# Attention and feed-forward on one core: leaner elementwise work in batches 0 and 1, one long second pass over the weights' last half, and fewer unread products

## The chip, the core and the metric

The kernel runs on 1 core of a Trainium2 chip. The time is device microseconds for one execution. The median of the three runs shown is 1007.32 us (1006.21 to 1008.86).

A core has five engines with a queue each: TensorE (PE in the profile; PEld is its weight load), VectorE (DVE), ScalarE (ACT), GpSimd (POOL) and SyncE (SP, which here issues most DMA transfers). Each queue is worked in the order in which the program was written. TensorE writes to PSUM, eight banks of 512 float32 columns; GpSimd does not touch PSUM in this kernel.

## What is computed

```python
# attention, for 8 batches x 8 heads, 576 tokens, 64 columns a head
q_d, k_d, v_d = (mean of q, k, v over each 4 rows)          # 144 rows
out_d = softmax(q_d @ k_d.T / 8) @ v_d                      # down-sampled part, repeated 4 times
scores = where(|i - j| < 4, q @ k.T / 8, -1e9)
out = repeat(out_d, 4) + softmax(scores) @ v                # local part in a band of 7
# feed-forward, on x = out as 4608 tokens x 512
h = x @ w_in                                                # 512 -> 2048
y = (h * cos(h)) @ w_out                                    # 2048 -> 512
```

Products of the feed-forward part are done in three passes with operands that are split into a high and a low half (names ending in `h` and `l`).

## The kernel before

**Feed-forward.** The 4608 tokens are 12 tiles of 384 (`t`), the 2048 hidden columns 16 chunks of 128 (`c`). A step (t, c) is `gemm1` (L727: 12 matmuls at L739 into one of two banks, then the activation on ScalarE and VectorE, L748 to L757, and the low half of its result at L399) and, two steps later, `gemm2` (L763: nine matmuls at L775 into three banks that collect over chunks). Tile 0 is made of batch 0's tokens alone; tile 1 holds the last 192 tokens of batch 0 and the first 192 of batch 1; tile 2 the rest of batch 1. `PASSES` (L36) sets the order of the steps: tiles 0 to 2 go through chunks 0 to 3, then 4 to 7, 8 to 11 and 12 to 15, since the weights are still arriving; from tile 3 on, each tile goes through all 16. At the end of each pass of a tile its three banks are evacuated (L791); the first pass stores its result, the later ones add to it with an accumulating DMA from GpSimd's queue (L800).

**Weights.** `w_load` (L402) brings 64-bit words, 512 KB for a chunk of one matrix; `w_split` (L412) makes the two float32 halves: one step on ScalarE (L420), four on VectorE (L421, L423, L425, L427), the high half (L431 or L432) and the low half (L399). 32 such splits are made. The buffers of the last chunks first hold data of the attention of batches 0 and 1.

**Attention** works on pairs of heads, four in a batch, in five functions. `u_qk` (L469) loads q and k and sums groups of four rows (L490 on VectorE, or L483 and L485 on GpSimd). `u_v` (L494) loads v in two layouts and sums its groups of four rows (L504, L505, on GpSimd or VectorE). `u_s` (L510) makes the scores and the softmax: local scores (L546) and down-sampled scores (L555) in two banks; VectorE adds the mask (L569), takes the maximum (L574) and subtracts it (L399); the down-sampled maximum is L582; ScalarE does the exponentials (L593 to L597); sums and reciprocals follow (L609 to L613), and the scaling by them at L615, on GpSimd or VectorE, or at L621 on ScalarE in four steps. `u_t` (L626) transposes: local on VectorE (L632), down-sampled on TensorE (L648) with evacuations at L465 or L466. `u_pv` (L654) multiplies by v: down-sampled at L665, local at L677 (L684 from batch 2 on); L696 adds the two, and L711 and L399 write the high and low half of x. The functions have another branch for batches from 2 on (`b >= NEARLY`).

**What sets the order.** No queue's order is written by hand. `Plan` collects all operations with an engine (or several), an assumed length and their dependencies, and a list scheduler (L165 to L279) sets them in an order and picks the engine. After that, where TensorE is assumed idle before an operation, the loop at L885 puts in products that nobody reads (L892, of 512 columns, bf16); in front of batch 0's operations at least `CFG["warm"]` of them. SyncE's loads for batches 0 and 1 and the weights are in a chain written by hand (L858), with three in flight at first.

## Time and profile before

| what | value |
|---|---|
| median of the runs shown | 1007.32 us |
| the profiled execution's own time | 1007.4 us |
| its span, first to last instruction | 1005.6 us |
| mean granted TensorE clock | 0.988 |
| PE, DVE, ACT, POOL busy | 981.2, 681.7, 610.2, 221.3 us |
| unread products (L892) | 125, 38.7 us busy |
| accumulating stores on GpSimd's queue (L800) | 27 of 256 KB |

The profile is one execution, recorded by instruction. Busy time of TensorE includes pipelining and unread products, so that 98% does not say that all of it was needed. "Idle before" with a name behind it is the time for which an engine stood, and the instruction that let it go on. "issue" is a wait for nothing that the profile shows. A matmul on float32 data leaves two records. In the chain of waits, an instruction is counted from where its predecessor in the chain ended, so its piece may be shorter than its duration in the timeline.

### The profile page before, as it was taken

To read this page: it belongs to the slowest core of one execution; us is meant where nothing else is said; L and a number is where in the kernel's file an instruction comes from. 1 tells how busy PE (TensorE), PEld (TensorE's weight loads), DVE (VectorE), ACT (ScalarE), POOL (GpSimd) and SP (SyncE) were. 2 spreads that over 40 slices of the span, in tenths; PEclk is the share of its full clock that TensorE was granted. 3 is DMA by queue.
4 is the path that set the end of the run, shared out by engine and by line. 5 is a ranking of instruction groups with operands and counts; after the bars stand their busy time and mean duration, and the time that the engine had idled before them with its cause. 6 is when DMAs were issued, how large, how long until landed. Compare 5 with 4: busy or idle time off the path is not lost.

```text
span 1005.6 us, 23855 instructions
## 1 busy us (share of the span) xinstructions
PE 981.2 (98%) x9917; PEld 847.3 (84%) x9917; DVE 681.7 (68%) x1362; ACT 610.2 (61%) x1174; POOL 221.3 (22%) x280
## 2 busy tenths in 40 slices
PE   8878999999999999999999999999999999999998
PEld 4546899899887888889888888888888888899997
DVE  7799899986587578464758957655657865433433
ACT  3457588876576656555547746654646665655554
POOL 6775325631153202000002211200001300000000
PEclk9979799999999999999999999999999999999999
DMA  7784643424355322210212312201112320100000
GB/s 224 234 270 149 215 159 64 80 36 68 67 116 132 78 65 70 68 33 28 81 49 71 129 49 58 83 26 36 62 54 73 112 65 4 37 1 1 32 1 32
DMA packets 41051, 80.70 MB, mean 80 GB/s; under 512 B 4976, under 2 KB 16240, under 8 KB 40944
## 3 DMA queue, kind: packets, MB, share of 16 engines
q1 hardware_dynamic: 37056, 72.11, 23.2%
q0 software_dynamic: 3888, 7.08, 5.0%
q8 instruction: 78, 1.28, 0.5%
q14 instruction: 29, 0.24, 0.1%
HBM read 57.93 MB, written 16.52 MB: 74 GB/s over the span
## 4 chain that ended last, share of the span: by engine, by line
PE 87%; DVE 6%; DMA 4%; issue 1%; ACT 1%; SPq 0%; ACTq 0%; DVEq 0%
PE bank L775 38%; PE bank L739 38%; PE bank L539 2%; PE bank L684 2%; PE bank L555 2%; PE bank L665 2%; PE bank L648 1%; DMA q<-qT 1%; DMA wdi<-w_in 1%; PE bank L892 1%; PE bank L677 1%; DMA vl<-vl 1%; DVE su L609 1%; DMA wxi<-qT 0%; DVE wxo L615 0%
## 5 line engine op out<-in xcount | busy, mean ns | idle before, releaser
L775 PE MATMUL bank<-wo,gh 128*128 128x512 f32 x1152 | 363.5, 396 | 0.0
L775 PEld LDWEIGHTS bank<-wo,gh 128*128 128x128 f32 x1152 | 210.0, 188 | 38.0 <-issue 3.1
L775 PE MATMUL bank<-wo,gl 128*128 128x512 f32 x576 | 227.6, 396 | 0.0
L750 ACT ACTIVATE tr<-bank,bmagic 128x384 f32<-128x384 f32 x192 | 110.9, 577 | 113.5 <-PE bank L739 109.7
L754 DVE SCALAR_TENSOR_TENSOR tr<-tr,bank 128x384 f32<-128x384 f32 x192 | 105.0, 547 | 108.0 <-ACT tr L749 107.1
L751 DVE SCALAR_TENSOR_TENSOR tr<-tr,bank 128x384 f32<-128x384 f32 x192 | 105.6, 550 | 84.2 <-ACT tr L750 83.2
L748 ACT ACTIVATE tr<-tr 128x384 f32<-128x384 f32 x192 | 100.7, 524 | 77.0 <-DVE tr L751 76.4
L756 ACT ACTIVATE gh<-tr 128x384 fp32r<-128x384 f32 x163 | 85.3, 523 | 88.3 <-DVE tr L754 86.8
L399 DVE TENSOR_TENSOR gl<-tr,gh 128x384 fp32r<-128x384 f32 x154 | 92.4, 600 | 63.5 <-ACT gh L756 60.5
L775 PEld LDWEIGHTS bank<-wo,gl 128*128 128x128 f32 x576 | 108.0, 187 | 23.5
L739 PE MATMUL bank<-x0h,wi 128*128 128x384 f32 x384 | 107.5, 340 | 0.0
L739 PE MATMUL bank<-x1h,wi 128*128 128x384 f32 x384 | 107.1, 339 | 0.0
L739 PE MATMUL bank<-x2h,wi 128*128 128x384 f32 x384 | 106.8, 338 | 0.0
L739 PE MATMUL bank<-x3h,wi 128*128 128x384 f32 x384 | 106.5, 338 | 0.0
L749 ACT ACTIVATE tr<-tr 128x384 f32<-128x384 f32 x192 | 100.8, 525 | 6.1
L399 POOL TENSOR_TENSOR gl<-tr,gh 128x384 fp32r<-128x384 f32 x38 | 43.0, 1132 | 269.6 <-DVE gh L757 175.8
L739 PEld LDWEIGHTS bank<-x0h,wi 128*128 128x128 f32 x384 | 70.5, 189 | 2.6 <-issue 0.5
L739 PEld LDWEIGHTS bank<-x1h,wi 128*128 128x128 f32 x384 | 70.3, 188 | 2.6 <-issue 0.6
L739 PEld LDWEIGHTS bank<-x2h,wi 128*128 128x128 f32 x384 | 70.2, 188 | 2.3 <-issue 0.4
L739 PEld LDWEIGHTS bank<-x3h,wi 128*128 128x128 f32 x384 | 70.2, 188 | 2.0
L739 PE MATMUL bank<-x0l,wi 128*128 128x384 f32 x192 | 64.6, 337 | 0.0
L739 PE MATMUL bank<-x3l,wi 128*128 128x384 f32 x192 | 64.6, 336 | 0.0
(199 smaller groups left out, 1452.6 us busy)
## 6 DMA issues: line engine op xcount, KB each, us to landing
vl<-vl SPq DMA_DIRECT2D x26, 384.0 KB
out<-ob SPq DMA_DIRECT2D x36, 256.0 KB
wdi<-w_in SPq DMA_DIRECT2D x16, 512.0 KB
wdo<-w_out SPq DMA_DIRECT2D x16, 512.0 KB
q<-qT SPq DMA_DIRECT2D x26, 292.0 KB
k<-kT SPq DMA_DIRECT2D x26, 292.0 KB
vd<-vdn SPq DMA_DIRECT2D x26, 288.0 KB
out<-ob POOLq DMA_DIRECT2D x27, 256.0 KB, 5.2
```

Of the source, the lines that this page charges most:

```text
L399: f = lambda e: lambda: e.tensor_tensor(out=out(), in0=in0(), in1=in1(), op=ALU.subtract)
L539: pe.matmul(banks[h].get()[BS * g:BS * (g + 1), c:c + BS], q.get()[hs, o:o + BS], k.get()[hs, o:o + BS], start=True, stop=True)
L555: pe.matmul(banks[h].get()[:HD, i * SD:(i + 1) * SD], qkd.get()[hs, 0, i * HD:(i + 1) * HD], qkd.get()[hs, 1, :], start=True, stop=True)
L665: pe.matmul(banks[0].get()[64 * h:64 * h + 64, 2 * SD:3 * SD], vd.get()[:, kh, 64 * h:64 * h + 64], ptd.get()[:, h, kh, :], start=(kh == 0 ...
L739: pe.matmul(ph.get()[:, :m], w[:, i, kc, :], x[:, kc, :], start=(n == 0), stop=(n == 3 * KC - 1))
L748: act.activation(tr.get(), tr.get(), AF.Sin, scale=PI)
L749: act.activation(tr.get(), tr.get(), AF.Square)
L750: pl.op("ACT", _act(m, True, 1), lambda: act.activation(tr.get(), h(), AF.Identity, bias=bmagic), r=[ph], w=[tr])
L751: pl.op("DVE", _dve(m), lambda: dve.scalar_tensor_tensor(out=tr.get(), in0=tr.get(), scalar=MAGIC, in1=h(), op0=ALU.subtract, op1=ALU.subt ...
L754: pl.op("DVE", _dve(m), lambda: dve.scalar_tensor_tensor(out=tr.get(), in0=tr.get(), scalar=0.5, in1=h(), op0=ALU.subtract, op1=ALU.mult), ...
L756: pl.op("ACT", _act(m, False), lambda: act.activation(gh.get(), tr.get(), AF.Copy), r=[tr], w=[gh], alts=[("DVE", _dve(m / 2), lambda: dve ...
L775: pe.matmul(o, (gh, gh, gl)[k].get()[:, sl], wo.get()[:, (0, 1, 0)[k]], start=(c == c0 and k == 0), stop=(c == c1 - 1 and k == 2))
```

## The change

All of it concerns batches 0 and 1, except `PASSES`.

- `PASSES`: tiles 0 to 2 now go through chunks 0 to 3, 4 to 7 and then 8 to 15 in one stretch.
- `warm` is 1 instead of 2: in front of batch 0's attention operations on TensorE stands at least one unread product.
- The mask is bf16, and TensorE puts it into the bank as a product with the identity ahead of the local scores, which are added to it. VectorE's mask addition goes; the maximum and the subtraction read PSUM, in halves of 192 columns, both on VectorE.
- The sum of v's groups of four rows goes; instead the down-sampled product takes all four rows of a group, in 16 matmuls where there were 4.
- The scaling of the down-sampled softmax is always on ScalarE.
- Three assumed lengths of the scheduler follow this (0.95 to 1.3, 0.64 to 2.1, and the scaling's).

```diff
-PASSES = [(t, c, c + NF) for c in range(0, NC, NF) for t in range(3)] + [(t, 0, NC) for t in range(3, NT)]
+PASSES = [(t, c, e) for c, e in ((0, NF), (NF, 2 * NF), (2 * NF, NC)) for t in range(3)] + [(t, 0, NC) for t in range(3, NT)]
...
-           fgap=0.4, f0=0.8, fend=300.0, warm=2)
+           fgap=0.4, f0=0.8, fend=300.0, warm=1)
...
-    mask = const.tile([P, NSEG + 1, BS], F32, name="mask")
+    mask = const.tile([P, NSEG + 1, BS], BF16, name="mask")
...
+        if b < NEARLY:
+            st[(b, pr)].update(vd=vd4, vl=vt)
+            return
         vd = ub(b, pr, "vd")
...
+            if b < NEARLY:
+                for h in range(2):
+                    pe.matmul(banks[h].get()[:, LQ:LQ + NSEG * BS], ident_b, mask[:, h:h + NSEG].rearrange("p s n -> p (s n)"),
+                              start=True, stop=False)
...
-                                  q.get()[hs, o:o + BS], k.get()[hs, o:o + BS], start=True, stop=True)
+                                  q.get()[hs, o:o + BS], k.get()[hs, o:o + BS], start=False, stop=(n % NSEG == NSEG - 1))
         if b < NEARLY:
-            pl.op("PE", 0.95, l_mm, r=[q, k], pw=banks, w=loc)
+            pl.op("PE", 1.3, l_mm, r=[q, k], pw=banks, w=loc)
...
+        if b < NEARLY:
+            for h in range(2):
+                mx = pl.buf(None)
+                using(banks[h], pl.op("DVE", _dve(NSEG * BS), lambda h=h: dve.tensor_reduce(
+                    out=segs(mxl, h), in_=lq(h), axis=AX.X, op=ALU.max), r=[loc[h]], pw=[mxl], w=[mx]))
+                using(banks[h], pl.op("DVE", _dve(NSEG * BS), lambda h=h: dve.tensor_tensor(
+                    out=segs(sml, h), in0=lq(h), in1=segs(mxl, h).unsqueeze(2).broadcast_to([P, NSEG, BS]), op=ALU.subtract),
+                    r=[loc[h], mx], pw=[sml]))
...
-                alts.append(("ACT", 4 * _act(SD, False, 1), scaled))
-            pl.op("POOL", _pool(size), f(pool), r=[su], w=[sm], alts=alts, shares=True)
+                pl.op("ACT", 4 * _act(SD, False, 2), scaled, r=[su], w=[sm])
+            else:
+                pl.op("POOL", _pool(size), f(pool), r=[su], w=[sm], alts=alts, shares=True)
...
+            if b < NEARLY:
+                for i in range(8):
+                    for h in range(2):
+                        pe.matmul(banks[0].get()[64 * h:64 * h + 64, 2 * SD:3 * SD], vd.get()[:, i, 64 * h:64 * h + 64],
+                                  ptd.get()[:, h, i // 4, :], start=(i == 0), stop=(i == 7))
+                return
...
-            pl.op("PE", 0.64, d_mm, r=[vd, ptd], pw=[banks[0]], w=[poo])
+            pl.op("PE", 2.1, d_mm, r=[vd, ptd], pw=[banks[0]], w=[poo])
```

In the changed program the lines have moved: the mask product is L538, the scores L553 and L562, the maximum and the subtraction L582 and L584, the down-sampled maximum L599, the scaling on ScalarE L638, the transposes L666, the down-sampled and the local product L684 and L701, the additions L720, `gemm1` and `gemm2` L763 and L799, the unread products L916.

More of the change, by code (lines that the diff above doesn't have):

```diff
@@ L567, in u_s @@
         pl.op("POOL", 0.15, lambda: pool.memset(su.get(), 1.0), w=[su])
-        for h in range(2):
-            using(banks[h], pl.op("DVE", _dve(NSEG * BS), lambda h=h: dve.tensor_tensor(
-                out=sml.get()[:, NSEG * h:NSEG * (h + 1)], in0=banks[h].get()[:, LQ:LQ + NSEG * BS].rearrange("p (s n) -> p s n", n=BS),
-                in1=mask[:, h:h + NSEG] if b < NEARLY else band, op=ALU.add), r=[loc[h]] + zeroed[:1], pw=[sml]))
         n = 2 * NSEG * BS
         bl = lambda t: t.unsqueeze(2).broadcast_to([P, 2 * NSEG, BS])
-        pl.op("DVE", _dve(n), lambda: dve.tensor_reduce(out=mxl.get(), in_=sml.get(), axis=AX.X, op=ALU.max), r=[sml], w=[mxl])
-        sub(n, sml.get, sml.get, lambda: bl(mxl.get()), r=[mxl], w=[sml])
+        segs = lambda t, h: t.get()[:, NSEG * h:NSEG * (h + 1)]
+        lq = lambda h: banks[h].get()[:, LQ:LQ + NSEG * BS].rearrange("p (s n) -> p s n", n=BS)
+        if b < NEARLY:
[8 more added lines that the diff above has]
+            for h in range(2):
+                using(banks[h], pl.op("DVE", _dve(NSEG * BS), lambda h=h: dve.tensor_tensor(
+                    out=segs(sml, h), in0=lq(h), in1=band, op=ALU.add), r=[loc[h]] + zeroed[:1], pw=[sml]))
+            pl.op("DVE", _dve(n), lambda: dve.tensor_reduce(out=mxl.get(), in_=sml.get(), axis=AX.X, op=ALU.max), r=[sml], w=[mxl])
+            sub(n, sml.get, sml.get, lambda: bl(mxl.get()), r=[mxl], w=[sml])
         mxd = sb("mxd", 2, [HD, 2, 2])
@@ L621, in scaled @@
                             act.activation(smd.get()[:, h, i], smd.get()[:, h, i], AF.Copy, scale=sud()[:, h, i:i + 1])
-                alts.append(("ACT", 4 * _act(SD, False, 1), scaled))
-            pl.op("POOL", _pool(size), f(pool), r=[su], w=[sm], alts=alts, shares=True)
+                pl.op("ACT", 4 * _act(SD, False, 2), scaled, r=[su], w=[sm])
+            else:
+                pl.op("POOL", _pool(size), f(pool), r=[su], w=[sm], alts=alts, shares=True)
         u["sml"], u["smd"] = sml, smd
@@ L662, in d_mm @@
         def d_mm():
+            if b < NEARLY:
+                for i in range(8):
+                    for h in range(2):
+                        pe.matmul(banks[0].get()[64 * h:64 * h + 64, 2 * SD:3 * SD], vd.get()[:, i, 64 * h:64 * h + 64],
+                                  ptd.get()[:, h, i // 4, :], start=(i == 0), stop=(i == 7))
+                return
             for kh in range(2):
```

## The prediction

> **What bounds the kernel now.** First the page: its busy table, and the chain that ended last.
>
> ```profile
> span 1005.6 us, 23855 instructions
> PE 981.2 (98%) x9917; PEld 847.3 (84%) x9917; DVE 681.7 (68%) x1362; ACT 610.2 (61%) x1174; POOL 221.3 (22%) x280
> PE 87%; DVE 6%; DMA 4%; issue 1%; ACT 1%; SPq 0%; ACTq 0%; DVEq 0%
> ```
>
> TensorE is on the chain for 87%, and the 6% of VectorE and 4% of DMA must lie where TensorE is not yet saturated. The chain of waits, asked for the first 115 us, shows where that ends.
>
> ```profile
> 32.56 0.25 PE bank L648 x4
> 34.05 0.54 PE bank L892 x2
> 34.59 1.52 PE bank L677 x96
> 106.19 1.82 PE bank L892 x4
> 108.00 1.37 PE bank L539 x91
> 109.38 1.17 PE bank L555 x8
> 110.54 2.46 PE bank L739 x12
> ```
>
> The first multiplication of token tile 1 starts at 110.54. It needs batch 1's attention, and four steps on tile 0 were already done by then. What TensorE still waits for after 115 us is, in the waits of PE:
>
> ```profile
> PE bank L684 <- DMA ptb<-sml: 1.5, 3, 0.9
> PE bank L648 <- DVE smd L615: 0.8, 1, 0.8
> PE bank L539 <- ACT ptd L465: 0.4, 1, 0.4
> ```
>
> That is 2.7 us in 890. So the time is 110.54 us of head, then fixed TensorE work; the change counts by what it does to 110.54, and by any new wait behind it. The busy time by stretch, cut where batch 0's last addition ends (46.84) and where batch 1's does (107.36); the columns are length, then busy us and instructions of PE, PEld, DVE, ACT and POOL, the granted clock, DMA share and GB/s:
>
> ```profile
> 0.00:46.84 46.84, 40.51 (x1033) 23.60 (x1035) 34.81 (x74) 18.68 (x65) 31.68 (x65) 0.96 0.76 232
> 46.84:107.36 60.52, 49.43 (x887) 34.70 (x888) 56.41 (x107) 37.94 (x97) 37.20 (x43) 0.86 0.66 212
> ```
>
> In the second stretch VectorE is busy for 56.4 of 60.5 us: it sets the pace. In the first it has 12 us free, and waits for TensorE at the end.
>
> **Batch 0.** The timeline shows TensorE from the first transposes, and VectorE's wait behind the last head pair.
>
> ```profile
> 18.34 0.42 PE L648 MATMUL bank<-ident,smd 72*72 72x72 f32 x4
> 36.83 0.56 PE L546 MATMUL bank<-k,q 64*32 64x32 f32 x40
> 37.68 0.68 PE L546 MATMUL bank<-k,q 64*32 64x32 f32 x56 [0.29 <-issue]
> 90.09 0.71 PE L665 MATMUL bank<-wxi 72*64 72x144 f32 x8
> 90.73 0.44 PE L739 MATMUL bank<-x0h,wi 128*128 128x384 f32 x1
> 43.95 0.29 ACT L465 ACTIVATE wxi<-bank 128x144 f32<-128x144 f32 x1 [3.94 <-PE bank L665]
> 44.27 0.46 DVE L696 TENSOR_TENSOR wxi<-bank,wxi 128x288 f32<-128x288 f32 x1 [4.24 <-ACT wxi L465]
> 46.39 0.45 DVE L696 TENSOR_TENSOR wxi<-bank,wxi 128x288 f32<-128x288 f32 x1
> ```
>
> The program order on TensorE near the end of batch 0, third head pair, before (L892 are the unread products, L665 the down-sampled product, L677 the local one, L546 batch 1's first scores):
>
> ```order
> L665 MATMUL bank<-wxi_200 64x144 x4
> L892 LDWEIGHTS ident_b
> L892 MATMUL bank<-ident_b 128x512
> ...
> L677 MATMUL bank<-wxo_390,wxi_502 64x24 x48
> ...
> L648 MATMUL bank<-ident,wxi_214 72x72 x4
> L546 MATMUL bank<-k,q 32x32 x48
> ```
>
> and now (L916, L684, L701 and L553 are the same four, L538 the new mask products):
>
> ```order
> L701 MATMUL bank<-wxo_395,wxi_554 64x24 x48
> L916 LDWEIGHTS ident_b
> L916 MATMUL bank<-ident_b 128x512
> L684 MATMUL bank<-wxi_202,wxo_487 64x144 x16
> ...
> L666 MATMUL bank<-ident,wxi_205 72x72 x4
> L538 LDWEIGHTS ident_b
> L538 MATMUL bank<-mask,ident_b 128x192
> ...
> L553 MATMUL bank<-k,q 32x32 x48
> ```
>
> The down-sampled product went from 4 matmuls to 16, behind the local one, with one unread product between steps instead of two. Four of these matmuls took 0.64 us (90.09 to 90.73), so 16 take at most 2.56; the lower bound is the transposes' rate, 4 records in 0.25, which makes 2.0 for 32 records. I take 2.3. A head pair then costs two transposes 0.50, four unread products at 0.27 (half of the 0.54 for two) 1.08, local 1.52, down-sampled 2.3: 5.4 us. Four pairs are 21.6; batch 1's first scores 1.2 (0.56 and 0.68), their mask products and one unread product 0.5 (no row has 192 columns; a 512-column one costs 0.27, so two masks lie between 0 and 0.54, and I take the proportion, 0.2): 23.3. Here nothing waits for the sum of the four value rows any more: it has gone from VectorE and GpSimd, where it stood in line ahead of the scalings that the transposes wait for. So I let TensorE run without a pause from 18.34, to 41.6. Then the evacuation of 0.3 and two additions of 0.9: batch 0 ends at 42.8, **4.0 us** before 46.84. At 2.0 per product it is 5.2, at 2.56 3.0, and with pauses like the 0.29 of `issue`, some of them in each pair, up to 2 less. The first mask products also wait until GpSimd has written the mask, which held nothing before; I cost that at 0, since 18.34 comes after the scores of all four pairs, and at about 1 if it doesn't hide.
>
> **Batch 1.** VectorE's order at the border before (L696 batch 0's last additions, L427/L399 weight splitting and low halves, L569 to L574 batch 1's first softmax):
>
> ```order
> L696 TENSOR_TENSOR wxi_568<-bank,wxi_560 128x3x96
> L427 SCALAR_TENSOR_TENSOR xxh<-wdi_385,xxh 128x512
> L427 SCALAR_TENSOR_TENSOR xxh<-wdo_449,xxh 128x512
> L696 TENSOR_TENSOR wxi_568<-bank,wxi_560 128x3x96
> L399 TENSOR_TENSOR wi_946<-xxh,wi_946 128x512
> L399 TENSOR_TENSOR wo_951<-xxh,wo_951 128x512
> L399 TENSOR_TENSOR x0l<-wxi_568,x0h 128x384
> L399 TENSOR_TENSOR x1l<-wxi_568,x1h 128x192
> L569 TENSOR_TENSOR sml<-bank,mask 128x192 x2
> ```
>
> and now (L720, L582, L584 and L599 are additions, maximum, subtraction and the down-sampled maximum):
>
> ```order
> L427 SCALAR_TENSOR_TENSOR xxh<-wdo_453,xxh 128x512
> L399 TENSOR_TENSOR x0l<-wxo_487,x0h 128x384
> L490 TENSOR_REDUCE qkd<-q 128x144
> L399 TENSOR_TENSOR wo_957<-xxh,wo_957 128x512
> L582 TENSOR_REDUCE mxl<-bank 128x6 x2
> L584 TENSOR_TENSOR sml<-bank,mxl 128x192 x2
> L490 TENSOR_REDUCE wxo_199<-wxo_820 128x144
> L720 TENSOR_TENSOR wxi_577<-bank,wxi_552 128x3x96 x2
> L599 TENSOR_REDUCE mxd<-bank 72x2
> ```
>
> Batch 1's first softmax has moved ahead of batch 0's last additions, into the 4.24 us in which VectorE stood. The costs in 46.84 to 107.36, by groups, and one single instruction of the timeline:
>
> ```profile
> L423 DVE TENSOR_SCALAR xxh<-xxh 128x512 int32<-128x512 int32 x8 | 5.7, 714 | 0.0
> L421 DVE TENSOR_SCALAR xxh<-xxh 128x512 f32<-128x512 f32 x8 | 4.0, 514 | 0.0
> L425 DVE SCALAR_TENSOR_TENSOR xxh<-wdo,xxh 128x512 int32<-128x512 int32 x4 | 3.3, 813 | 0.0
> L427 DVE SCALAR_TENSOR_TENSOR xxh<-wdo,xxh 128x512 int32<-128x512 int32 x3 | 2.0, 678 | 0.0
> L615 DVE TENSOR_TENSOR wxo<-wxo,su 72x576 f32<-72x576 f32 x1 | 2.8, 2806 | 0.0
> L615 DVE TENSOR_TENSOR wxi<-wxi,su 72x576 f32<-72x576 f32 (+1 forms) x3 | 2.6, 883 | 0.0
> L399 DVE TENSOR_TENSOR wxi<-wxi,mxl 128x384 f32<-128x384 f32 x2 | 2.4, 1189 | 0.0
> L569 DVE TENSOR_TENSOR wxi<-bank,mask 128x192 f32<-128x192 f32 x4 | 1.2, 348 | 1.4 <-PE bank L555 1.4
> L574 DVE TENSOR_REDUCE mxl<-wxi 128x12 f32<-128x384 f32 x2 | 1.1, 536 | 0.0
> L504 POOL TENSOR_TENSOR wxi<-wxi 72x512 f32<-72x512 f32 x2 | 3.2, 1600 | 4.3 <-DMA wxi<-vdn 4.3
> 80.20 0.41 DVE L423 TENSOR_SCALAR xxh<-xxh 128x512 int32<-128x512 int32 x1
> ```
>
> Gone from VectorE here: four scalings 5.4 (2.8 and 2.6, one of them a smaller one that moves to GpSimd), four subtractions 3.4 (2.4, and two at 0.5), eight mask additions 2.4 (twice the row), four maxima 2.1, low halves now done elsewhere about 1.4: 14.7. New: six maxima and six subtractions of 192 columns at the mask row's 0.35 (0.27 if a row's overlap with the next is taken off, 0.44 as the 288-column maximum), 4.2; and the order puts three more weight splits ahead of batch 1's end, 3 x (0.51 + 0.71 + 0.81 + 0.68) = 8.1; casts and one reduction 2.4: 14.7. So it is even: the time won is filled with splits that come due earlier.
>
> What remains is relief. One scaling cost 2.81 us beside GpSimd where three averaged 0.88. Five sums of value rows leave GpSimd, by the 1600 row and a second addition of some 0.8 at most 12 of its 37.2 us, a third. What staying rows lose to it (L423 at 0.71 where the single one took 0.41, 8 x 0.3, and by estimate as much again twice over in the other rows) is some 8 us; a third is **2.6 us**, bounds 0 and 5. [...]
>
> ScalarE gets three more scalings in four steps, beside 37.9 us busy of 60.5; the rows for it, and for TensorE at half clock:
>
> ```profile
> 57.09 1.33 ACT L621 ACTIVATE smd<-smd,su 72x144 f32<-72x144 f32 x4 [3.00 <-DVE su L613]
> 103.41 2.77 PE L677 MATMUL bank<-wxi,wxo 32*64 32x24 f32 x96
> 102.25 1.23 PE L665 MATMUL bank<-wxo 72*64 72x144 f32 x8
> 57.55 1.49 PE L648 MATMUL bank<-ident,smd 72*72 72x72 f32 x8 [4.02 <-ACT smd L621]
> 104.00:106.00 2.00, 2.00 (x84) 2.00 (x80) 1.02 (x3) 0.00 (x0) 0.00 (x0) 0.50 0.52 188
> ```
>
> The scalings are 3 x 1.33 = 4.0 us more on ScalarE, which is idle for 22; the transposes wait for each. Last, the tail from batch 1's last addition to 110.54 took 3.2 us, the three rows at 106.19 to 109.38, at a granted clock of 0.50 (last row). At full clock they would take half of the 4.4 us that they run for, which leaves 1.0 to 1.5 behind the last addition; I take half of that gain, **1.0 us**.
>
> **Sum.** 4.0 + 2.6 + 1.0 = 7.6. The profiled execution took 1007.4 (span 1005.6 and 1.8 around it; the median shown is 1007.32), so I predict **999.8**. Behind 110.54, nine accumulating stores and their nine evacuations go: they hang on no TensorE wait above, worth 0 (2.7 either way, the waits that are there).
>
> **Rivals.** (a) *VectorE stays as slow and ScalarE queues*: no relief, no tail gain, and each of batch 1's four scalings waits behind one split step of 0.67. Then 4.0 - 2.7 = 1.3: 1006.1. For it: VectorE at 93%. Against: GpSimd's third is certain. (b) *Half clock in batch 0*, the one that ends slower. With half the unread products TensorE may lose its clock. At half clock the local product takes 2.77 against 1.52, the down-sampled one 1.23 against 0.64, and 1.82 is four unread ones. A pair then costs 1.0 + 1.8 + 2.8 + 4.4 = 10.0 instead of 5.4, the whole chain 23.3 x 1.85, 19.8 more. If two thirds of it run so, 13.2 more less 7.6 is 5.6: 1013.0; it decides from 38% of the chain on. Against: the bigger product keeps TensorE busier. [...] (c) *Chunks 12 to 15 come too late*: tile 0 now wants chunk 12 at step 28, not 36. Eight splits at 2.7 us, were none done ahead, are 21.6 of waiting less 7.6: 1021.3; it decides where VectorE falls a whole lead behind. Against it: the order puts chunk 12's split behind 17 steps' activations, chunk 15's behind 26 of 31, and 110 to 222 us ran with VectorE at 103.3 of 112:
>
> ```profile
> 110.00:222.00 112.00, 112.00 (x717) 100.63 (x714) 103.30 (x190) 91.00 (x171) 47.73 (x46) 1.00 0.42 109
> ```
>
> There the order has 22 splits in 27 steps, (103.3 - 22 x 2.7) / 27 = 1.6 us a step for the rest; now it has 19 in 22 steps, 19 x 2.7 + 22 x 1.6 = 86.5 of 91.3, 95% against 92%: tight, with a lead of 5 to 11 steps.
>
> **Chances.** Forecast 0.65, from 993.5 (product at 2.0, relief 5, the whole tail 2, and some 1.7 of VectorE's 4.1 idle: 13.9) to 1004.3; rival (a) 0.18 and mixtures of it and (b) 0.02, within 0.3% (3.0 us, about what a measurement here can tell); (b) 0.11 and (c) 0.04 slower. Range 993.5 to 1007.5, which takes in (a) and leaves out (b) and (c).
>
> **What would show it.** Right: token tile 1's first product near 103; batch 0's last addition near 42.8; the 16-matmul product at 2.0 to 2.6; GpSimd at 25 of the stretch; the same 895 us behind. Wrong: granted clock under 0.9 before 42; L666 waiting for ScalarE's scaling; a wait of TensorE on a split between steps 24 and 33.

## The result, and the profile after

The changed program took 1015.26 us at the median of 20 executions (1003.05 to 1022.62), the program before 1005.09 us (20 executions, 1001.51 to 1012.01). The ratio is 1.005, 95% interval 1.0028 to 1.0072; executions over 1.5% above the fastest of the same program are left out of the ratios here and below (seven of these 20, the profiled one among them, and three of e10's six), and the other 13 have a median of 1011.2. So it is slower. The 20 times go with TensorE's mean granted clock: 1003.05 at 0.995, 1005.45 at 0.990, 1009.39 at 0.987, 1014.09 at 0.980, 1020 to 1022.6 at 0.972 to 0.975.

The page of the profiled execution (1022.5 us):

```profile
span 1020.7 us, 24129 instructions
PE 1000.7 (98%) x10085; PEld 868.7 (85%) x10085; DVE 673.4 (66%) x1363; ACT 610.5 (60%) x1187; POOL 186.7 (18%) x236
```

VectorE lost 8.3 us of work and GpSimd 34.6, as the change intends; TensorE is 19.5 us busier, with 29 fewer unread products before its first step on tile 0 (44 for 73). The stretches, cut as before at the last additions of batches 0 and 1 (columns as there: length, busy us of PE, PEld, DVE, ACT, POOL, clock, DMA share, GB/s):

```profile
0.00:66.70 66.70, 59.21 (x1117) 42.56 (x1118) 33.47 (x84) 22.71 (x77) 17.70 (x47) 0.68 0.65 194
66.70:121.60 54.90, 50.59 (x970) 37.95 (x968) 51.64 (x116) 39.73 (x106) 25.01 (x25) 0.94 0.66 219
```

Batch 0 ends at 66.70 instead of 46.84 (+19.9), batch 1's stretch takes 54.9 instead of 60.5 (-5.6). Tile 1's first product starts at 123.89; the tail before it is 2.3 instead of 3.1, and what follows is 896.8 for 895.1. The sum, +15.1, is the difference of the spans. Batch 0 loses more than the whole of it, at a granted clock of 0.68. TensorE there:

```profile
18.43 0.96 PE L553 MATMUL bank<-wxo,wxi 64*32 64x32 f32 x89 [1.48 <-issue]
20.51 0.41 PE L666 MATMUL bank<-ident,smd 72*72 72x72 f32 x4
24.83 2.34 PE L701 MATMUL bank<-sml,vl 32*64 32x24 f32 x78 [2.77 <-issue]
27.64 4.11 PE L684 MATMUL bank<-ptd,vd 72*64 72x144 f32 x32
34.80 2.77 PE L701 MATMUL bank<-wxi,wxo 32*64 32x24 f32 x96
63.64 1.24 PE L562 MATMUL bank<-qkd 64*72 64x144 f32 x8
64.81 2.74 PE L916 MATMUL bank<-ident_b 128*128 128x512 bf16 x6
```

The down-sampled product takes 4.11 us and the local one 2.77; rival (b) had them at 4.4 and 2.8. Behind the first transposes (20.51) a pause of 2.77 us for `issue` (which no instruction released) stands inside a local product. VectorE's softmax of batch 1, which the order had moved ahead, came no earlier:

```profile
64.95 0.36 DVE L584 TENSOR_TENSOR sml<-bank,mxl 128x192 f32<-128x192 f32 x1 [6.22 <-PE bank L562]
65.89 0.81 DVE L720 TENSOR_TENSOR wxi<-bank,wxi 128x288 f32<-128x288 f32 x2
```

It waited 6.22 us for L562, which stands on TensorE behind the fourth pair's large product.

The clock of this stretch in windows of 3.41 us, cut where it changes (from 23.54 to 67.91 are 13 such windows):

```profile
20.13:23.54 3.41, 1.94 (x33) 1.21 (x30) 2.99 (x10) 2.90 (x13) 0.11 (x1) 1.00 0.72 186
23.54:26.96 3.42, 2.13 (x78) 2.12 (x77) 1.01 (x4) 3.42 (x16) 0.00 (x0) 0.50 0.72 188
26.96:30.37 3.41, 3.41 (x31) 2.88 (x29) 0.00 (x0) 0.01 (x1) 0.00 (x0) 0.50 0.77 222
...
33.78:37.19 3.41, 3.41 (x97) 2.88 (x97) 3.28 (x10) 1.88 (x5) 0.11 (x1) 0.50 0.88 278
37.19:40.61 3.42, 3.42 (x39) 2.91 (x37) 1.37 (x4) 0.79 (x3) 0.11 (x1) 0.50 0.68 182
...
61.09:64.50 3.41, 3.41 (x30) 2.93 (x27) 0.00 (x0) 0.29 (x1) 0.22 (x1) 0.50 0.02 8
64.50:67.91 3.41, 3.41 (x12) 1.61 (x9) 2.96 (x8) 1.18 (x4) 0.60 (x1) 0.50 0.00 0
67.91:71.33 3.42, 3.42 (x18) 2.25 (x17) 3.42 (x10) 2.52 (x12) 3.26 (x4) 1.00 0.46 120
```

It goes from 1.00 to 0.50 between two windows, stays there for 13 of them, and returns after the one that holds six unread products and the first steps. In eleven of the 13 TensorE was busy from end to end, and after ten of these the clock stayed at 0.50: being busy did not bring it back. The same windows for the unread products alone (PE and PEld busy, clock, DMA):

```profile
26.96:30.37 3.41, 0.61 (x1) 0.11 (x1) 0.50 0.77 222
...
61.09:64.50 3.41, 0.00 (x0) 0.00 (x0) 0.50 0.02 8
64.50:67.91 3.41, 2.74 (x6) 0.72 (x6) 0.50 0.00 0
```

The ten fully busy windows held mostly matmuls on 32 to 72 rows and columns (`64*32`, `72*72`, `32*64`, `72*64` and `64*72` in TensorE's rows above), and at most 1.25 us of matmuls on `128*128`.

### The profile page after: what moved, and what is told of

It reads as the page before. It is cut to its first block, busy times and chain, and to the rows that moved or that the text cites. A ratio compares the mean times of both kernels' runs of the same rounds, so it can differ in the third digit from the quotient of the medians.

```text
span 1020.7 us, 24129 instructions
## 1 busy us (share of the span) xinstructions
PE 1000.7 (98%) x10085; PEld 868.7 (85%) x10085; DVE 673.4 (66%) x1363; ACT 610.5 (60%) x1187; POOL 186.7 (18%) x236
## 4 chain that ended last, share of the span: by engine, by line
PE 75%; DVE 4%; DMA 2%; ACT 1%; SPq 1%; issue 1%; POOL 0%; ACTq 0%; DVEq 0%; POOLq 0%
PE bank L799 34%; PE bank L763 33%; PE bank L546 2%; PE bank L708 2%; PE bank L562 1%; PE bank L689 1%; PE bank L666 1%; DMA k<-kT 1%; SPq L657 1%; DMA ptb<-sml 1%; DMA q<-qT 1%; DVE tr L778 0%; DVE xxh L423 0%; DVE xxh L425 0%; DVE su L626 0%
## 5 line engine op out<-in xcount | busy, mean ns | idle before, releaser
L799 PE MATMUL bank<-wo,gh 128*128 128x512 f32 x1152 | 363.8, 397 | 0.0
L799 PEld LDWEIGHTS bank<-wo,gh 128*128 128x128 f32 x1152 | 209.7, 188 | 38.4 <-issue 3.6
L799 PE MATMUL bank<-wo,gl 128*128 128x512 f32 x576 | 227.7, 396 | 0.0
L778 DVE SCALAR_TENSOR_TENSOR tr<-tr,bank 128x384 f32<-128x384 f32 x192 | 104.9, 547 | 110.4 <-ACT tr L773 109.5
L780 ACT ACTIVATE gh<-tr 128x384 fp32r<-128x384 f32 x155 | 81.2, 524 | 89.8 <-DVE tr L778 88.4
L799 PEld LDWEIGHTS bank<-wo,gl 128*128 128x128 f32 x576 | 108.0, 187 | 23.5
L763 PE MATMUL bank<-x0h,wi 128*128 128x384 f32 x384 | 107.5, 340 | 2.3 <-DVE tr L778 2.3
L763 PE MATMUL bank<-x1h,wi 128*128 128x384 f32 x384 | 107.1, 339 | 1.0 <-DVE tr L778 1.0
L763 PE MATMUL bank<-x2h,wi 128*128 128x384 f32 x384 | 106.9, 339 | 1.1 <-DVE tr L778 1.1
L763 PE MATMUL bank<-x3h,wi 128*128 128x384 f32 x384 | 106.5, 338 | 0.0
L399 POOL TENSOR_TENSOR gl<-tr,gh 128x384 fp32r<-128x384 f32 x36 | 43.2, 1200 | 248.9 <-DVE gh L781 176.8
L763 PEld LDWEIGHTS bank<-x0h,wi 128*128 128x128 f32 x384 | 70.4, 188 | 6.3 <-DVE tr L778 3.2
L763 PEld LDWEIGHTS bank<-x1h,wi 128*128 128x128 f32 x384 | 70.3, 188 | 3.9 <-DVE tr L778 1.8
L763 PEld LDWEIGHTS bank<-x2h,wi 128*128 128x128 f32 x384 | 70.3, 188 | 3.2 <-DVE tr L778 1.4
L763 PEld LDWEIGHTS bank<-x3h,wi 128*128 128x128 f32 x384 | 70.2, 188 | 2.0
L763 PE MATMUL bank<-x0l,wi 128*128 128x384 f32 x192 | 64.6, 336 | 0.0
L763 PE MATMUL bank<-x1l,wi 128*128 128x384 f32 x192 | 64.5, 336 | 0.0
```

Of the source, the lines that this page charges most:

```text
L399: f = lambda e: lambda: e.tensor_tensor(out=out(), in0=in0(), in1=in1(), op=ALU.subtract)
L763: pe.matmul(ph.get()[:, :m], w[:, i, kc, :], x[:, kc, :], start=(n == 0), stop=(n == 3 * KC - 1))
L778: pl.op("DVE", _dve(m), lambda: dve.scalar_tensor_tensor(out=tr.get(), in0=tr.get(), scalar=0.5, in1=h(), op0=ALU.subtract, op1=ALU.mult), ...
L780: pl.op("ACT", _act(m, False), lambda: act.activation(gh.get(), tr.get(), AF.Copy), r=[tr], w=[gh], alts=[("DVE", _dve(m / 2), lambda: dve ...
L799: pe.matmul(o, (gh, gh, gl)[k].get()[:, sl], wo.get()[:, (0, 1, 0)[k]], start=(c == c0 and k == 0), stop=(c == c1 - 1 and k == 2))
```

## The experiments

First the numbers of all programs. "Ends" are where the last additions of batches 0 and 1 end, "PE" and "DVE" the busy time up to the latter, "tile 1" the start of its first product, "behind" the span from there. Ratios are against the program before on the same chip, which had medians of 1003.7 to 1006.0.

| program | median us | ratio, 95% interval | end 0 | end 1 | PE | DVE | tile 1 | behind |
|---|---|---|---|---|---|---|---|---|
| before | 1005.1 | | 46.8 | 107.4 | 89.9 | 91.2 | 110.5 | 895.1 |
| changed | 1015.3 | 1.0050 (1.0028-1.0072) | 66.7 | 121.6 | 109.8 | 85.1 | 123.9 | 896.8 |
| e12, changed again | 1011.0 (one) | | 55.0 | 110.3 | 99.0 | 85.0 | 113.4 | 895.8 |
| e1, changed, two products | 1012.6 | 1.0065 (1.0044-1.0086) | 53.1 | 109.5 | 97.1 | 85.1 | 112.6 | 898.9 |
| e2, before, one product | 1005.8 | 1.0001 (0.9987-1.0016) | 48.4 | 104.8 | 88.7 | 89.4 | 107.7 | 893.8 |
| e3, changed, old passes | 1018.1 | 1.0123 (1.0090-1.0156) | 52.8 | 111.9 | 101.5 | 85.4 | 114.8 | 902.2 |
| e4, before, new passes | 1008.5 | 1.0022 (1.0002-1.0041) | 47.4 | 105.5 | 88.2 | 91.3 | 109.9 | 896.9 |
| e5, changed, old product | 1011.4 | 1.0070 (1.0041-1.0099) | 50.7 | 109.4 | 93.5 | 90.3 | 113.9 | 896.4 |
| e6, before, larger product | 1020.7 | 1.0157 (1.0126-1.0187) | 58.0 | 118.7 | 108.0 | 85.3 | 120.8 | 903.1 |
| e7, before, mask part | 1014.6 | 1.0102 (1.0074-1.0129) | 45.2 | 102.3 | 87.0 | 87.4 | 107.0 | 903.2 |
| e8, changed, four products | 1019.1 | 1.0137 (1.0104-1.0170) | 58.4 | 116.7 | 106.3 | 85.1 | 119.5 | 897.3 |
| e9, before, quarter products | 1006.9 | 1.0012 (0.9991-1.0033) | 48.6 | 108.5 | 92.0 | 88.3 | 111.5 | 896.9 |
| e10, changed, 128 columns | 1028.1 | 1.0127 (1.0088-1.0167) | 56.9 | 119.5 | 108.2 | 85.9 | 122.5 | 897.4 |
| e11, mask, scaling | 1015.2 | 1.0097 (1.0076-1.0117) | 46.2 | 104.5 | 92.0 | 85.1 | 109.5 | 902.7 |
| e13, eight in a row | 1010.2 | 1.0049 (1.0023-1.0075) | 55.1 | 111.4 | 99.6 | 84.9 | 114.5 | 895.2 |
| e14, mask, new passes | 1005.5 | 0.9999 (0.9976-1.0021) | 45.5 | 101.7 | 89.0 | 85.2 | 106.4 | 896.4 |
| e15, mask, scaling, new passes | 1006.8 | 1.0011 (0.9984-1.0038) | 43.6 | 103.8 | 90.7 | 90.7 | 108.4 | 894.7 |
| e16, as e15, larger product in batch 1 | 1010.0 | 1.0042 (1.0018-1.0067) | 45.4 | 106.8 | 95.0 | 86.4 | 109.2 | 896.2 |
| e17, as e16, scaling free | 1009.1 | 1.0038 (1.0015-1.0060) | 46.8 | 111.0 | 96.9 | 87.8 | 113.7 | 893.9 |

### Unread products and passes: e1 to e4

My theory A was rival (b): too few unread products, half clock. B was the larger product, C a cause behind tile 1.

```diff
-           fgap=0.4, f0=0.8, fend=300.0, warm=1)
+           fgap=0.4, f0=0.8, fend=300.0, warm=2)
```

> The changed kernel with two unread products instead of one in front of batch 0's steps. Theory A (the time was lost because TensorE fell to half clock in batch 0, for want of unread products): the granted clock stays at 1.00 for nearly all of 20 to 45 us, batch 0's last addition ends at 44 to 49 us, the first product of token tile 1 at 103 to 107, time 0.994 to 0.999 of before. Theory B (the bigger down-sampled product, which fills half of the array, and the stalls for instructions bring the half clock whatever the unread products are): clock still 0.50 for over half of 25 to 60, time 1.000 to 1.010 of before. Theory C (the cause lies behind 124 us, in the longer pass): head well under before's 110.5, and yet no gain.

Measured: 1012.57 (ratio in the table). The clock was kept through most of batch 0, as its two stretches show:

```profile
0.00:53.13 53.13, 45.84 (x1139) 30.25 (x1139) 33.44 (x84) 22.70 (x77) 17.72 (x47) 0.97 0.77 234
53.13:109.50 56.37, 51.25 (x968) 38.95 (x968) 51.61 (x116) 39.68 (x106) 24.52 (x25) 0.92 0.67 222
```

Clock 0.97, and batch 0 still ends 6.3 us later than before. So half clock is not the whole loss, and A as I had put it falls. The reverse edit on the program before:

```diff
-           fgap=0.4, f0=0.8, fend=300.0, warm=2)
+           fgap=0.4, f0=0.8, fend=300.0, warm=1)
```

> The kernel before with one unread product instead of two. Theory A: half clock appears in batch 0 here too, for 10 us or more beyond before's, batch 0's last addition past 50, time 1.003 to 1.012 of before, and spread wider. Theory B: batch 0 gets some 4 us shorter on TensorE at full clock, time 0.996 to 1.000 of before.

1005.81, no difference in time. The clock went all the same, as A said, and batch 0 ended at 48.4:

```profile
0.00:48.36 48.36, 41.29 (x1010) 25.55 (x1011) 34.09 (x74) 19.09 (x65) 32.52 (x64) 0.83 0.80 237
```

That is half clock for 16.0 us, where the program before has 3.4, and over the 12 executions the median clock is 0.983, for 0.988 before on the same chip. Fewer unread products did let the clock go; the shorter chain on TensorE, which B counted on, pays for it. Then `PASSES` alone, undone in the changed program and done in the one before:

```diff
-PASSES = [(t, c, e) for c, e in ((0, NF), (NF, 2 * NF), (2 * NF, NC)) for t in range(3)] + [(t, 0, NC) for t in range(3, NT)]
+PASSES = [(t, c, c + NF) for c in range(0, NC, NF) for t in range(3)] + [(t, 0, NC) for t in range(3, NT)]
```

> The changed kernel with the passes of before (chunks 8 to 11, then 12 to 15). Theories A and B: the passes matter by 2 us or less, so it stays at 1.003 to 1.010 of before with half clock in batch 0. Theory C: it comes to 1.000 or under.

> The kernel before with the new passes alone. Theories A and B: within 0.2% of before, nine accumulating stores fewer and no TensorE wait for a weight split. Theory C: 1.003 or more of before, with waits of TensorE on weight splits between steps 24 and 33.

1018.12 and 1008.52. The new passes cost the program before some 2 us (0.2 to 4.1 by the interval), and the changed program is worse without them, by waits and 3.4 us of lost clock behind tile 1 (902.2). C falls: of the 15.1 us between the two profiles 1.7 lie behind tile 1.

### One part undone, one part alone: e5 to e7

```diff
-        if b < NEARLY:
-            st[(b, pr)].update(vd=vd4, vl=vt)
-            return
...
-            if b < NEARLY:
-                for i in range(8):
...
-            pl.op("PE", 2.1, d_mm, r=[vd, ptd], pw=[banks[0]], w=[poo])
+            pl.op("PE", 0.64, d_mm, r=[vd, ptd], pw=[banks[0]], w=[poo])
```

> The changed program with v's groups of four rows summed as before and the down-sampled product back at 4 matmuls; everything else of the change stays, one unread product in front of batch 0's steps too. Theory P (the 16-matmul product is the cause: its 1.5 us more in each of the eight head pairs lie on TensorE's chain of batch 0, 5.9 us, and it is narrow work that lets the clock go): batch 0's last addition at 44 to 48, a median of 1000 to 1005. Theory W (too few unread products let the clock go, whatever the product is): half clock in batch 0 stays, last addition beyond 52, median 1008 to 1015. Theory M (the mask products delay the first scores and split the stream into pauses): median 1008 to 1012, with TensorE waiting for the mask and for issue.

The same lines with the signs turned, on the program before, are e6:

> The program before with only one part of the change: v's sum of four rows goes and the down-sampled product takes 16 matmuls; two unread products, the old passes, the old mask addition and scaling stay. Theory P: batch 0's last addition 5 to 6 us later than 46.8, batch 1's stretch 1 to 4 us shorter (VectorE and GpSimd lose the sums), a median of 1007 to 1012. Theories W and M: nothing lost by this part, the sums' relief is won, 1001 to 1005.

e5: 1011.43, batch 0 ends at 50.7, with half clock from 30.2 to 43.8 and 47.2 to 54.1. The end is later than theory P said and earlier than W, the median inside W and M: no theory alone fits. e6: 1020.74, batch 0 ends 11.2 us later. TensorE got 18.1 us busier up to the end of batch 1 and VectorE 5.9 less busy; the two stretches of e6:

```profile
0.00:58.01 58.01, 51.76 (x1124) 34.14 (x1125) 34.10 (x75) 20.59 (x68) 27.50 (x57) 0.83 0.75 223
58.01:118.73 60.72, 56.24 (x959) 44.29 (x959) 51.17 (x109) 34.14 (x91) 27.84 (x33) 0.78 0.64 210
```

So the larger product does harm with two unread products too, more than I expected. In the second stretch TensorE is now the fuller engine (56.2 of 60.7, VectorE 51.2), though by estimate 13.3 us of that are lost clock (0.78).

```diff
+                    pe.matmul(banks[h].get()[:, LQ:LQ + NSEG * BS], ident_b, mask[:, h:h + NSEG].rearrange("p s n -> p (s n)"),
+                              start=True, stop=False)
...
+                using(banks[h], pl.op("DVE", _dve(NSEG * BS), lambda h=h: dve.tensor_reduce(
+                    out=segs(mxl, h), in_=lq(h), axis=AX.X, op=ALU.max), r=[loc[h]], pw=[mxl], w=[mx]))
```

> The program before with only the mask part of the change: the bf16 mask as a product ahead of the local scores, maximum and subtraction from PSUM in halves of 192 columns; two unread products, the old passes, sums and scaling stay. Theory M: 1 to 3 us later in batch 0, with a wait on the mask ahead of the first scores, median 1006 to 1010. Theory P: VectorE is relieved of some 0.6 us a head pair and TensorE pays 0.2 to 0.3, median 1000 to 1005.

1014.62, but not where M said: batch 0 and tile 1 come 1.7 and 3.5 us earlier, and 8.1 are lost behind. VectorE's timeline there:

```profile
309.88 0.75 DVE L490 TENSOR_REDUCE qkd<-q 128x144 f32<-128x576 f32 x1 [3.87 <-DMA q<-qT]
314.92 0.74 DVE L629 TENSOR_TENSOR smd<-smd,su 72x576 f32<-72x576 f32 x1
```

and TensorE's:

```profile
315.81 1.15 PE L662 MATMUL bank<-ident,smd 72*72 72x72 f32 x8 [3.86 <-DVE smd L629]
```

VectorE stands for a load of q, the scaling queues behind it, TensorE waits 3.86 us for that (0.8 for the same scaling before) and then runs two windows of 3.41 us at half clock (314.8 to 321.7). A gain at 107 us can be given back at 312.

### What lets the clock go, and what holds it: e8 to e10, e12, e13

Four unread products per step in the changed program:

```diff
-           fgap=0.4, f0=0.8, fend=300.0, warm=1)
+           fgap=0.4, f0=0.8, fend=300.0, warm=4)
```

> The changed program with four unread products in front of batch 0's steps instead of one. Theory W: clock 1.00 through batch 0, and the forecast gain appears: median 998 to 1004. Theory P: the clock is up (mean 0.99 or more), but the products stand on the same chain: three times some 20 steps at 0.27 each are up to 16 us where TensorE has no gap, so batch 0 ends no earlier than with two (53.1), median 1010 to 1020.

1019.05: full clock through batch 0, which ends at 58.4. P was right here: kept by four products per step, the clock costs more than it brings.

The pauses for `issue` lie at regular places. Counted in records of TensorE from the start, they stand in the changed program at 347 and 474, in its second execution (e12) at 222, 347, 474 and 729: steps of 125 to 128 or twice that. The changed program's page has a line for the queue that brings instructions (packets, megabytes, share):

```profile
q8 instruction: 79, 1.29, 0.5%
```

This is 16 KB a packet; with the second such queue 1.53 MB for 24129 instructions, 63 bytes each, so by estimate a packet holds some 257 instructions: 128 matmuls and their weight loads. I take the pauses for waits for the next block of code: each of these ends 1.3 to 1.6 us after such a packet has come in (16.93 and 18.43, 23.31 and 24.83 in the changed program; 10.30 and 11.75, 15.78 and 17.33, 19.84 and 21.27, 31.68 and 33.02 in e12). To test whether they halve the clock, e9 cuts each unread product in front of batch 0's steps into four:

```diff
-                    pe.matmul(s[2].get(), ident_b, ident_b.unsqueeze(1).broadcast_to([P, 4, P]), start=True, stop=True)
+                    for j in range(4 if ahead else 0):
+                        pe.matmul(s[2].get()[:, j * P:(j + 1) * P], ident_b, ident_b, start=True, stop=True)
...
```

> The program before with each unread product in front of batch 0's steps cut into four of 128 columns: the same columns through TensorE, four times the instructions. Theory F (a stream of many short instructions runs ahead of the loading of its own code, stands for 'issue' at steps of about 128 matmul records, and after such a pause the clock is halved): pauses for issue before 60 us grow from 2.2 us to 4 or more, half clock follows them by 1 to 2 us, batch 0's last addition comes 3 us or more later than 46.8, median 1007 to 1013. Theory H (only narrow work lets the clock go, pauses or not): no more half clock than before, median 1003 to 1006.

TensorE's waits up to the end of batch 0 (us in total, times, longest):

```profile
PE bank L546 <- issue: 2.7, 3, 1.3
PE bank L677 <- issue: 2.0, 2, 1.3
PE bank L648 <- issue: 0.3, 1, 0.3
```

and the window up to there:

```profile
0.00:48.57 48.57, 41.01 (x1230) 34.28 (x1230) 34.14 (x74) 19.02 (x65) 32.66 (x65) 1.00 0.77 232
```

The pauses grew from 1.7 to 5.0 us, as theory F said, but the clock stayed at 1.00 and the time is the same (ratio 1.0012). Pauses alone, between the 128x128 work of this program, did not halve it. e10 widens the 16 matmuls:

```diff
-                        pe.matmul(banks[0].get()[64 * h:64 * h + 64, 2 * SD:3 * SD], vd.get()[:, i, 64 * h:64 * h + 64],
+                        pe.matmul(banks[h].get()[:, 2 * SD:3 * SD], vd.get()[:, i, :],
```

> The changed program with each of the 16 matmuls of the down-sampled product 128 columns wide instead of 64: both heads' columns of v are multiplied, the half that belongs to the other head is not read, and each head has a bank of its own, with one evacuation more per pair. The same number of matmuls at the same 63 ns a record, twice the columns of the array at work. Theory H: the clock is kept in batch 0, median clock 0.988 or more, median time 1005 to 1010. Theory F: the same pauses and half clock as in the changed program, median clock 0.976 to 0.984, median time 1011 to 1018.

The first of these products in TensorE's timeline:

```profile
25.84 4.09 PE L684 MATMUL bank<-ptd,vd 72*128 72x144 f32 x32
```

1028.06 and of no use for its question: my premise that the duration stays was wrong. At full clock the 16 matmuls take 4.09 us with 128 columns, 2.18 with 64 (next fence), so the two heads' halves had run two at a time: in the trace of e12 they start in pairs, 0.006 us apart, and the next pair 0.12 us later.

e12 is the changed program as it is:

> The changed program as it is, one more execution, to see where the time lies in another of its runs. Theory F: pauses for issue lie again near the 348th and 479th matmul record or a multiple of about 128 away, their lengths differ from the first profile, and the end of batch 0 follows the length of half clock (about 0.8 us for each us of clock lost). Theory H: half clock from 24 to 67 us again, whatever the pauses.

TensorE's timeline in this execution, to the pause ahead of its half clock:

```profile
17.33 0.96 PE L553 MATMUL bank<-wxo,wxi 64*32 64x32 f32 x89 [0.93 <-issue]
19.42 0.41 PE L666 MATMUL bank<-ident,smd 72*72 72x72 f32 x4
21.27 1.35 PE L701 MATMUL bank<-sml,vl 32*64 32x24 f32 x78 [0.30 <-issue]
22.88 2.18 PE L684 MATMUL bank<-ptd,vd 72*64 72x144 f32 x32
33.02 0.26 PE L666 MATMUL bank<-ident,wxo 72*72 72x72 f32 x1 [1.28 <-issue]
```

The pauses stand at the same places (x89 and x78) with other lengths; half clock lasts from 35.28 to 55.76, six windows instead of 13, so H's 24 to 67 did not come again. Half of the half-clock time up to the end of batch 0 I count as clock lost, an estimate from the granted 0.50: 21.6 us of 43.2 in the first execution, 9.9 of 19.8 here. Without it batch 0 would end at 45.1 in both. So by this count the 11.7 us between these two ends of batch 0 are lost clock. Its 1011.0 is close to the 1011.2 above. Its two stretches:

```profile
0.00:55.03 55.03, 48.22 (x1117) 34.28 (x1118) 33.38 (x84) 22.70 (x77) 17.64 (x47) 0.82 0.76 234
55.03:110.33 55.30, 50.76 (x969) 38.07 (x968) 51.64 (x116) 39.83 (x106) 24.50 (x25) 0.93 0.63 208
```

In the 19 profiles of the table I read 118 changes of the clock between 6 and 134 us from windows of 1 us. In each profile all of them lie a multiple of 3.41 us apart, within 0.05. Sorting TensorE's rows into these steps, each matmul counted from its start to the next one's: each of the 59 halvings follows a step with at least 0.35 us without a matmul and at most 1.5 us of 128x128 work; but of 169 steps with 0.4 us idle or more only 58 were followed by half clock. Half-clock steps that were followed by another held 0.64 us of 128x128 work in the mean, those followed by full clock 2.14. Whether wide work is what counts, e13 tests, with eight unread products in a row ahead of each local product:

```diff
-                for _ in range(max(n, CFG["warm"] if ahead else 0)):
+                for _ in range(max(n, (8 if abs(o.dur - 1.52) < 1e-6 else CFG["warm"]) if ahead else 0)):
```

> The changed program with eight unread products in a row in front of each head pair's local product in batch 0 (28 more in all, where two per step added about 20), one elsewhere. In the profiles so far the clock changes only at steps of 3.41 us, each halving follows a step with at least 0.4 us of idle time on TensorE, and every half-clock step with more than 1.82 us of 128x128 work is followed by full clock. Theory H (wide work in a step of 3.41 us brings the clock back): eight at half clock are 3.5 us, so each half-clock spell in batch 0 lasts at most 4 steps (13.7 us) instead of up to 13, median clock 0.985 to 0.992; the products themselves cost 28 x 0.22 = 6.2 us on the chain, batch 0 ends at 51 to 58, median 1006 to 1013. Theory N (what holds the clock down is the narrow product itself): spells of 20 us and more stay, median clock 0.980, median 1015 to 1022.

Three steps of 3.41 us around its only half clock in batch 0, then the rest of batch 0:

```profile
16.09:19.50 3.41, 1.60 (x100) 1.19 (x98) 3.37 (x12) 1.49 (x5) 0.12 (x1) 1.00 0.97 312
19.50:22.92 3.42, 3.42 (x20) 2.25 (x20) 1.61 (x4) 1.18 (x4) 0.11 (x1) 0.50 0.80 261
22.92:26.33 3.41, 3.41 (x106) 2.17 (x104) 2.78 (x10) 3.32 (x16) 0.00 (x0) 1.00 0.87 259
26.33:55.05 28.72, 26.50 (x587) 18.77 (x586) 16.22 (x38) 11.34 (x33) 9.49 (x15) 1.00 0.74 224
```

One step of half clock, then full clock to the end of batch 0, and a median clock of 0.992: the spell is as short as theory H said. The same narrow products ran here at full clock; N falls. But the first eight products start only 0.15 us before that step ends:

```profile
22.77 1.97 PE L916 MATMUL bank<-ident_b 128*128 128x512 bf16 x8
```

So e13 shows that the clock was held with this 128x128 work (1.00 from 22.92 to 55.05), not that the work brought it back. Full clock also came back without any 128x128 work, after this step of e2 (transposes of 72x72, scores of 64x32 and 64x144):

```profile
59.66:63.07 3.41, 3.41 (x111) 2.60 (x110) 2.87 (x4) 1.42 (x4) 3.25 (x5) 0.50 1.03 334
```

Of the 59 returns, 11 followed a step with less than 1.2 us of it. Rows of the array in use, times columns sent through, added up over the matmul records of a step, fit better: one limit, 365 thousand, sorts 135 of the 145 half-clock steps rightly, where the best limit on the time of 128x128 work sorts 120. That limit was chosen afterwards, no run tests it, and e2's step is among its ten misses.

The 28 further products stand on the chain, at 0.22 each 6.2 us, and batch 0 ends at 55.1 as in e12: what the clock brings is paid away (1010.22, a ratio of 1.0049 for 1.0050).

### Sums of parts: e11, e14 to e17

e11 is the changed program with `warm=2`, the old passes and the old product (the diffs above); e14 is e7 with the new passes; e15 is e11 with the new passes.

> The changed program without the larger product (v's sums and 4 matmuls as before), without the new passes, and with two unread products: what is left is the mask as a product and the scaling on ScalarE. If the product, the passes and the fewer unread products are what costs, and the rest is the relief that I forecast: batch 0's last addition at 43 to 46, batch 1's stretch 1 to 3 us shorter, median 999 to 1004. If the denser stream alone is enough for pauses and half clock: median 1007 to 1014, as for the mask alone.

> The program before with the mask part and the new passes together; two unread products, sums, 4 matmuls and the scaling as before. The mask alone brought tile 1's first product from 110.5 to 107.0 and lost 8 us behind it, 3.9 of them in one wait of batch 2's transposes at 312 us, which no program with the new passes has shown. If that wait belongs to the old passes: tile 1 at 106 to 108, 895 to 898 behind, median 1002 to 1006. If it belongs to the mask part (VectorE's order): again 900 or more behind, median 1008 to 1014.

> The changed program with only the larger product and the fewer unread products undone: mask product, scaling on ScalarE and new passes, v's sums and 4 matmuls, two unread products. If the product and the unread products carry the loss and the wait at 312 us goes with the new passes: batch 0's last addition near 46, tile 1's first product at 107 to 110, 895 to 898 behind, median 1002 to 1007. If not: 1009 to 1015.

1015.16, 1005.46, 1006.81. e11 has e7's wait (3.6 us on the scaling of batch 2, 902.7 behind); with the new passes it is gone in both, 896.4 and 894.7 behind. e6, with the old passes and no mask part, has one of 4.3 us too, so the mask part is not needed for it. It was seen only with the old passes, and there not in all programs: e2 and e9 keep the 0.8 us of before. e14 and e15 start tile 1 4.1 and 2.1 us earlier than before, and their profiled executions have 2.8 and 2.6 us less span, but over all executions the ratios are 0.9999 and 1.0011. Without the larger product the change is worth nothing either way; with it (e1, two products as well) the ratio goes from 1.0011 to 1.0065. Last, the larger product where I thought that it pays, in batch 1 alone:

```diff
-        if b < NEARLY:
+        if b == 1:
             st[(b, pr)].update(vd=vd4, vl=vt)
...
-            if b < NEARLY:
+            if b == 1:
                 for i in range(8):
```

> The changed program with the larger product in batch 1 alone (batch 0 has v's sums and 4 matmuls again) and two unread products. Theory: the larger product costs 1.47 us a head pair where TensorE sets the pace (batch 0) and saves some 5 us where VectorE does (batch 1, whose stretch was 54.9 and 55.3 us in the changed program against 60.5 before and 60.2 with the product undone). Then batch 0's last addition is at 43 to 46, batch 1's stretch 55 to 57 us, tile 1's first product at 102 to 105, 895 to 897 behind, median 999 to 1003. If batch 1's shorter stretch came from something else, or goes lost to half clock: 1005 to 1008.

e17 is e16 with the scaling as before:

```diff
-                pl.op("ACT", 4 * _act(SD, False, 2), scaled, r=[su], w=[sm])
-            else:
-                pl.op("POOL", _pool(size), f(pool), r=[su], w=[sm], alts=alts, shares=True)
+                alts.append(("ACT", 4 * _act(SD, False, 1), scaled))
+            pl.op("POOL", _pool(size), f(pool), r=[su], w=[sm], alts=alts, shares=True)
```

> The same with the scaling free to go to GpSimd, VectorE or ScalarE as before: mask product, new passes and the larger product in batch 1 alone, two unread products. If the scaling on ScalarE is worth nothing, as e14 and e15 side by side say (1005.5 and 1006.8): within 2 us of the run beside it, median 999 to 1004. If it gives VectorE room in batch 1: 2 to 4 us slower than that run.

1009.95 and 1009.13: both miss, though they lie 0.8 us apart, as e17 has it for a scaling that is worth nothing. Batch 1's stretch in e15:

```profile
43.64:103.78 60.14, 52.04 (x933) 37.12 (x933) 57.08 (x118) 38.94 (x105) 31.58 (x35) 0.87 0.71 236
```

and in e16:

```profile
45.40:106.80 61.40, 55.08 (x979) 41.61 (x978) 54.97 (x121) 39.66 (x106) 27.53 (x34) 0.86 0.73 238
```

VectorE has 2.1 us less to do, TensorE 3.0 more, and the stretch is 1.3 longer. The relief is real and does not count, since TensorE is as full. No version here beats the program before.

## Why the prediction was wrong

**Batch 0 is the step that failed:** "So I let TensorE run without a pause from 18.34", at full clock, -4.0 us. The prices in it were right: the product at full clock 2.11 (22.88 to the next row at 24.99; I took 2.3), local 1.53, a pair 5.8 with a pause of 0.30 in it (19.42 to 25.22) for 5.4. But the first transposes came at 19.42 and 20.51, behind pauses for `issue` and the wait for the mask, which I had at 0 or about 1; in e12:

```profile
PE bank L538 <- POOL mask L341: 1.4, 1, 1.4
```

Without lost clock batch 0 would end at 45.1, -1.7, and the program before has one half-clock step there too (42.57 to 45.98), so that at equal clock the gain lies between 0 and 1.7. On top come 9.9 or 21.6 us of lost clock, so +8.2 and +19.9.

**Rival (b) is what happened**, to which I gave 0.11. My reason against it, that the bigger product keeps TensorE busier, took busy time for what keeps the clock: ten fully busy windows stayed at 0.50. Its condition, too few unread products, is borne out by the clocks of all executions: a median of 0.9805 in the changed program, 0.990 with two products (e1); 0.988 before, 0.983 with one (e2). The larger product did it as well: e6, with two, has 19.9 us of half clock in batch 0 and a median clock of 0.981. Why e1, which has that product too, keeps its clock is not shown. That the rival's 1013.0 is near the 1015.26 is in part luck. It took 13.2 us of lost clock less 7.6 of gain. Span times clock takes the lost clock off an execution, by estimate; the median of this is 994.9 us for the changed program and 991 to 993 for the program before beside the experiments. So some 7 to 8 of the 10.2 us at the median are lost clock, and the rest is longer work: the gain did not come either.

**Batch 1** was forecast at -2.6, by VectorE alone, bounds 0 and 5 (what I called some 8 us of loss adds up to 7.2, a third of it to 2.4). VectorE did what I said: three more splits are in the stretch (L421 and L423 eleven times for eight), and its busy time fell by 4.8, the relief being nearer its upper bound if the work was counted rightly. Two groups of VectorE in the changed program's stretch:

```profile
L421 DVE TENSOR_SCALAR xxh<-xxh 128x512 f32<-128x512 f32 x11 | 5.7, 523 | 0.0
L423 DVE TENSOR_SCALAR xxh<-xxh 128x512 int32<-128x512 int32 x11 | 5.6, 508 | 0.0
```

L423 went from 714 to 508 ns with GpSimd at 25.0 us (forecast 25). The stretch got 5.6 us shorter (5.2 in e12), but that is mostly the clock, which I read for the tail alone: at 0.86 the stretch lost 8.5 us before, at 0.94 and 0.93 it loses 3.6 and 3.8. Without lost clock it is 52.0 us before, 51.3 and 51.5 after. VectorE's relief hardly shortened it. Against it stand four products of 1.47 us more, for which I charged TensorE nothing in batch 1: lost clock taken off, TensorE is busy for 47.0 us there instead of 40.9, and its idle time went down by about as much (11.1 to 4.3). It is now nearly as full as VectorE (50.6 and 51.6 of 54.9 us, clock included), and e16 shows a relief that goes to waste in the same way with batch 0 at its old length. Which of the two engines sets the end of batch 1 was not separated.

**The rest.** The tail of -1.0 was -0.8, and 0 in e12. Behind tile 1, +1.7 and +0.6 lie in my 2.7 either way. Rival (c) did not come: no wait on a split behind tile 1, and the passes alone cost some 2 us (e4). Of rival (a) little is seen: in batch 1 TensorE waits 1.2 us for the scaling on ScalarE in e12 and 1.6 in e1, where the program before waited 4.0 for its one, and e14 and e15, without and with it, don't differ.

The added terms of e12 are +8.2, -5.2, 0 and +0.6: 3.6 us of span. What in a step decides the clock is open: 58 of 169 steps with idle time were followed by half clock, and I found no threshold that separates them all.

## What to carry to other kernels

Moving elementwise work into matmuls paid nothing here where TensorE had little room (in batch 1 it was busy for 50.6 of 54.9 us), so add its busy time up to the point that counts, not only the time of the engine that is relieved. On a chain of matmuls on a part of the array the granted clock was one of the terms: a pause of 2.77 us came with 13 steps at 0.50, by estimate 21.6 us of lost clock in batch 0. So look at the clock of each 3.41 us and at how many rows of the array work in it, for how many columns; that count sorted 135 of 145 half-clock steps, with a limit chosen afterwards. Read the clock of a stretch before you put its change in length down to an engine's relief. Unread products that hold the clock had a price where nothing else covered them, 0.22 us each in e13 (eight in a row took 1.89 us).

## What was unexpected of the hardware

- The granted clock changed only at multiples of 3.41 us (118 changes in 19 profiles), and stayed at 0.50 for 13 such steps in the changed program, though TensorE was busy throughout eleven of them.
- A dense stream of small matmuls stood for `issue`, as I read it for its own code, 125 to 128 matmul records apart or a multiple, 0.3 to 2.8 us at a time, at the same places and with other lengths in another execution (0.93 and 0.30 for 1.48 and 2.77).
- Two 64-column matmuls ran side by side: 16 in 2.18 us, against 4.09 us with 128 columns each.
